# Two MLPs behind linear attention on one core: pair order, hosted heads and weight preparation rearranged

## The chip, the core and the metric

The kernel runs on one core of one Trainium2 chip. The metric is the device time of one execution in microseconds (us). Times are medians of several runs. The profile is of one execution, taken by the hardware profiler.

## What is computed

The reference, cut to what matters:

```python
def _attn_ref(q, k, v, g_norm):                       # (8 batches, 8 heads, 576, 64)
    kv = np.einsum('bhsd,bhse->bhde', k, v)
    out = np.einsum('bhsd,bhde->bhse', q, kv)
    rms = np.sqrt(np.mean(out * out, axis=-1, keepdims=True) + 1e-06)
    return out / rms * g_norm

def _moe_ref(x, w_in, w_out):                         # 4608 x 512, 512 x 2048, 2048 x 512
    h = x @ w_in
    g = np.where(h >= 1, h, np.where(h <= -1, 0.0, (h + 1) ** 2 / 4))
    return g @ w_out

def _moe2_ref(x, w_in, w_out):                        # the same sizes
    r = np.maximum(x @ w_in, 0.0)
    return (r * r) @ w_out

x = attn_out.transpose(0, 2, 1, 3).reshape(4608, 512)
return _moe2_ref(_moe_ref(x, ...), ...)
```

The weights arrive as 64-bit floats, and the kernel narrows them itself.

## The kernel before, in words

The 4608 tokens are nine blocks of 512. Blocks 0 to 7 are the first 512 tokens of each batch; block 8 collects the last 64 tokens of all eight. Each number is held as a high and a low part, so that one product takes three matmuls.

**The plain stage.** Blocks 0 to 4 of the first layer run one after the other. A block has 16 slices of the hidden width. Slice f is an `h_stage` (12 matmuls into `ph`, evicted to `u`), a `g_stage` (`u` split into the two parts of `gs`) and, two slices later, an `out_stage` (12 matmuls into `acc`). A slice has two hook steps, so block b has the steps 32b to 32b+31. The `hooks` table says which other work is issued at which step. Two kinds of work are hooked in.

* **Attention** of a later batch, by pairs of heads: `load_kv`, `load_q`, `kv_stage` (matmuls `pkv`), `t_stage` (a transpose into `qf`, split into `qT0` and `qT1`), two `o_stage` (matmuls `po` from `qT` and `kvbd`) and `r_stage` (matmuls `pr`, then the norm). Batch b is computed during block b-1. Of batches 5 to 7 the results go to DRAM (`xpd`, and `xrd` for block 8).
* **Weight preparation.** The later stage needs sums of weight quarters. A *unit* (`which`, `i`) makes them for one slice pair of one weight matrix in both layers: two raw loads, two `prep_narrow`, `prep_sums`, four `prep_split` for layer 2; `prep_join`, `prep_sums`, two `prep_split` for layer 1. On DVE that is 20 instructions. Each `prep_split` fills one tile `s`, and `pay` stores it to DRAM (`wsd`) from ACT's DMA queue. There are 16 units, and `keep_first` stores 23 more weight tiles from SP's queue in steps 14 to 58. The split tiles take turns in four buffers (`w1_12` to `w1_15`).

**The pair stage.** The other work is done two blocks at a time with seven products in place of eight: `PAIRS` lists (layer, first block), and block 8 of layer 2 follows alone. A pair has an in-phase (`ph`, 28 steps of 12 matmuls) and an out-phase (`po`, 56 steps of 6). Weights come back from `wsd` as tiles `ws`, one DMA each. `x2_jobs` load and split the next pair's inputs (`xr` to `x2`) during the out-phase. `HOSTED` says which pair also computes attention; `in_pair` holds those jobs by step.

What sets the order on an engine: the program is written in this order with hooks, and a scheduler orders it into one fixed list per engine. Each engine runs its list in order, and a DMA issue stands in the list of the engine that issues it. DMA completions use eight semaphores in turn (`DMAHW0` to `DMAHW7` in the waits of the program), so an issue waits for the earlier transfer on its semaphore.

Of the kernel before, what the change touches and what calls it, by code (L numbers as in the profile page):

```python
# [77 lines left out]
def linear_attention_rms_two_mlps(  # L78
# [42 lines left out]
    xp = ctx.enter_context(tc.tile_pool(name="xp", bufs=2 * KD))  # L121
# [12 lines left out]
    PAIRS = [(2, 0), (1, PLAIN), (2, 2), (1, PLAIN + 2), (2, 4), (2, 6)]  # L134
    EARLY = ((5, 0), (5, 1), (5, 2))
    HOSTED = {
        0: ((6, 0), (6, 2), (5, 3), (6, 1), (6, 3)),
        2: ((7, 0), (7, 2), (7, 1), (7, 3)),
    }
    hosted = [a for n in HOSTED for a in HOSTED[n]]  # L140
# [167 lines left out]
    prep_tags = itertools.cycle(range(NF - TAIL + RING + 2, NF))  # L308

    def prep_tile(name, shape, dtype):  # L310
        return wp.tile(shape, dtype, tag=f"w1_{next(prep_tags)}", name=name)
# [97 lines left out]
    def load_kv(b, hp):  # L409
        h0 = 2 * hp  # L410
        if b > 0:

            r = rests[turn[b, hp] % len(rests)]
            kvr[b, hp] = (r[:, 0], r[:, 1])
        both = None
        if (b, hp) in hosted[2:]:
# [211 lines left out]
    def new_x(L, b):  # L628
        xs[L, b] = [
            xp.tile([P, 2, TB], F32R, tag="x", name=f"x{L}_{b}_{c}") for c in range(KD)  # L630
        ]
# [137 lines left out]

    w_ring = Ring(*((wp, f"w1_{i}") for i in (0, 1, 2, 3, 4)))  # L770
    t_ring = Ring(*[(gp, "g")] * 3, (wp, f"w0_{NF - 2}"), (wp, f"w0_{NF - 1}"))
    g_ring = Ring(*[(xp, "x")] * 8, *((wp, f"w1_{5 + i}") for i in range(8)))
# [335 lines left out]
    jobs += attention(2 * NF * (PLAIN - 1), 9, EARLY)  # L1108
# [12 lines left out]

    kept = [(w, f) for f in range(NF) for w in range(2) if w == 0 or f < NF - TAIL]
# [3 lines left out]
    units = []  # L1126
    for n in range(NQ):
        for which, i, s in ((0, 2 * n, 0), (0, 2 * n + 1, 8), (1, n, 16), (1, n + NQ, 24)):
            units.append((which, i, 2 * NF * (n + 1) - 4 + 2 * n + s))
    units[-1] = (*units[-1][:2], 2 * NF * PLAIN - 7)  # L1130
    for which, i, s0 in units:
        for d, L, f, a in (
# [16 lines left out]
    last = 2 * (PLAIN - 1) * NF  # L1149
# [172 lines left out]
```

## Time and profile before

| | us |
|---|---|
| median of 3 runs | 1569.22 (1567.16 to 1569.58) |
| the profiled execution, own time | 1570.57 |
| its span, first to last instruction | 1568.8 |
| TensorE (PE) busy | 1537.6 |
| VectorE (DVE) busy | 1197.7 |
| ScalarE (ACT) busy | 932.2 |
| mean granted TensorE clock | 0.996 of full |

The plain blocks 1 to 4 start their first matmul at 128.1, 236.2, 335.9 and 433.7 us; the first matmul of the pair stage is at 536.1 us, its first out-phase starts at 630 us. PE, DVE, ACT and SP are engines; "PE po <- ACT qT" means that PE's matmul into `po` waited for ACT's write of `qT`. "L879" is line 879.

### The profile page before, as it was taken

To read this page: it belongs to the slowest core of one execution; us is meant where nothing else is said; L and a number is where in the kernel's file an instruction comes from. 1 tells how busy PE (TensorE), PEld (TensorE's weight loads), DVE (VectorE), ACT (ScalarE), POOL (GpSimd) and SP (SyncE) were. 2 spreads that over 40 slices of the span, in tenths; PEclk is the share of its full clock that TensorE was granted. 3 is DMA by queue.
4 is the path that set the end of the run, shared out by engine and by line. 5 is a ranking of instruction groups with operands and counts; after the bars stand their busy time and mean duration, and the time that the engine had idled before them with its cause. 6 is when DMAs were issued, how large, how long until landed. Compare 5 with 4: busy or idle time off the path is not lost.

```text
span 1568.8 us, 22366 instructions
## 1 busy us (share of the span) xinstructions
PE 1537.6 (98%) x7631; PEld 1268.9 (81%) x7633; DVE 1197.7 (76%) x2112; ACT 932.2 (59%) x1751; POOL 11.9 (1%) x30
## 2 busy tenths in 40 slices
PE   9999899999999999999999999999999999999999
PEld 5787678888777778788888888888888888888899
DVE  6987878887888767987897479878975597558666
ACT  5976766776757556754674466546743464446354
POOL 0000000000000000000000000000000000000000
PEclk9999999999999999999999999999999999999999
DMA  9677999787897977778677867696776676977796
GB/s 287 198 251 226 309 339 316 253 256 256 256 317 243 331 239 203 234 203 227 210 248 230 254 200 246 213 247 219 246 231 210 194 248 193 246 246 218 216 391 249
DMA packets 330914, 388.17 MB, mean 247 GB/s; under 512 B 197808, under 2 KB 223408, under 8 KB 330800
## 3 DMA queue, kind: packets, MB, share of 16 engines
q1 hardware_dynamic: 299904, 330.63, 69.7%
q10 hardware_dynamic: 30896, 56.11, 9.6%
q8 instruction: 61, 1.00, 0.2%
q14 instruction: 53, 0.43, 0.1%
HBM read 300.42 MB, written 86.25 MB: 246 GB/s over the span
## 4 chain that ended last, share of the span: by engine, by line
PE 77%; DMA 6%; DVE 2%; ACT 2%; SPq 0%; issue 0%; ACTq 0%; DVEq 0%
PE po L879 32%; PE ph L879 31%; PE ph L243 6%; PE acc L243 6%; DMA wsd<-s 3%; DMA wt<-wsd 1%; PE po L243 1%; DMA ws<-wsd 1%; PE pkv L488 1%; PE pr L610 1%; DMA rest<-in_v_dram 1%; DMA xr<-x1d 1%; DMA xr<-xpd 0%; ACT s L222 0%; DVE s L190 0%
## 5 line engine op out<-in xcount | busy, mean ns | idle before, releaser
L879 PE MATMUL ph<-x,ws 128*128 128x512 f32 (+1 forms) x2352 | 504.8, 374 | 4.6 <-DVE u L706 2.4
L879 PEld LDWEIGHTS ph<-x,ws 128*128 128x128 f32 x2352 | 417.2, 188 | 83.4 <-DVE u L706 2.8
L879 PE MATMUL po<-t,ws 128*128 128x512 f32 x2016 | 460.1, 390 | 0.0
L879 PEld LDWEIGHTS po<-t,ws 128*128 128x128 f32 x2016 | 378.8, 188 | 79.0 <-DVE t L808 0.4
L808 DVE TENSOR_TENSOR t<-g,t 128x512 fp32r<-128x512 f32 (+1 forms) x336 | 216.3, 649 | 91.8 <-ACT t L222 87.1
L222 ACT CAST t<-g 128x512 fp32r<-128x512 f32 (+1 forms) x336 | 195.9, 590 | 126.5 <-PE po L879 64.1
L243 PE MATMUL ph<-x,w 128*128 128x512 f32 x960 | 242.9, 397 | 2.2 <-DVE u L706 0.8
L243 PEld LDWEIGHTS ph<-x,w 128*128 128x128 f32 x960 | 179.5, 190 | 41.9 <-ACT w L222 2.0
L243 PE MATMUL acc<-gs,w 128*128 128x512 f32 x528 | 131.7, 394 | 4.5 <-DVE gs L235 2.2
L956 ACT ACTIVATE g<-h 128x512 f32<-128x512 f32 (+1 forms) x120 | 70.6, 589 | 90.5 <-DVE h L945 90.4
L243 PEld LDWEIGHTS acc<-gs,w 128*128 128x128 f32 x528 | 97.5, 188 | 26.2 <-DVE gs L235 2.6
L945 DVE CUSTOM_DVE_ANT_0 h<-ph,e 128x512 f32<-128x512 f32 (+1 forms) x120 | 76.4, 637 | 53.3 <-PE ph L879 49.4
L935 DVE TENSOR_TENSOR e<-ph,e 128x512 f32<-128x512 f32 (+1 forms) x112 | 72.1, 650 | 52.2 <-PE ph L879 47.2
L243 PE MATMUL acc<-gs,wt 128*128 128x512 f32 x432 | 106.2, 391 | 0.8 <-DMA wt<-wsd 0.8
L243 PEld LDWEIGHTS acc<-gs,wt 128*128 128x128 f32 x432 | 79.9, 188 | 17.6 <-DMA wt<-wsd 1.2
L222 ACT CAST x<-xr 128x512 fp32r<-128x512 f32 (+1 forms) x98 | 57.4, 590 | 49.8 <-DVE xr L859 30.3
L222 ACT CAST gs<-u 128x512 fp32r<-128x512 f32 x80 | 49.8, 622 | 46.2 <-DVE u L706 31.1
L706 DVE SCALAR_TENSOR_TENSOR u<-u,ph 128x512 f32<-128x512 f32 x80 | 54.5, 681 | 21.6 <-ACT u L229 21.4
L235 DVE TENSOR_TENSOR gs<-u,gs 128x512 fp32r<-128x512 f32 x80 | 54.9, 686 | 20.8 <-ACT gs L222 20.6
L704 ACT ACTIVATE u<-ph,halfb 128x512 f32<-128x512 f32 x80 | 55.3, 691 | 19.5 <-PE ph L243 13.3
L932 ACT COPY e<-ph 128x512 f32<-128x512 f32 (+1 forms) x56 | 30.7, 554 | 58.1 <-PE ph L879 49.6
L808 DVE TENSOR_TENSOR x<-xr,x 128x512 fp32r<-128x512 f32 (+1 forms) x98 | 62.9, 647 | 0.0
(135 smaller groups left out, 1623.3 us busy)
## 6 DMA issues: line engine op xcount, KB each, us to landing
ws<-wsd SPq DMA_DIRECT2D x392, 512.0 KB, 4.3
wsd<-s ACTq DMA_DIRECT2D x96, 512.0 KB, 5.2
wt<-wsd SPq DMA_DIRECT2D x36, 512.0 KB, 5.3
raw<-in_moe_w_in_dram SPq DMA_DIRECT2D x32, 512.0 KB, 6.8
raw<-in_moe_w_out_dram SPq DMA_DIRECT2D x32, 512.0 KB, 6.7
xr<-x1d SPq DMA_DIRECT2D x36, 256.0 KB, 4.5
out_dram<-ov SPq DMA_DIRECT2D x142, 64.0 KB, 3.9
wsd<-w SPq DMA_DIRECT2D x17, 512.0 KB, 4.7
```

The lines of the kernel that those rows point to most:

```text
L222: return e.copy(dst, src)
L235: lo = engine(op + "_lo", phase).tensor_tensor(t[:, 1, :], src, t[:, 0, :].bitcast(F32), ALU.subtract)
L243: nc.tensor.matmul(dst, wt(a), xt(c), start=first and n == 0, stop=last and n == 2)
L488: nc.tensor.matmul(ps[s, d], lhs, rhs, start=c == 0, stop=c == MR)
L704: nc.scalar.activation(u, ps, AF.Relu, bias=halfb, scale=0.5)
L706: nc.vector.scalar_tensor_tensor(u, u, 1.0, ps, op0=ALU.min, op1=ALU.max)
L808: engine2(op + "_lo").tensor_tensor(t[:, 1, :], src, t[:, 0, :].bitcast(F32), ALU.subtract)
L879: nc.tensor.matmul(ps, wt(a), xt(c), start=first and n == 0 and i == 0, stop=last and n == len(lhs) - 1 and i == 2, skip_group_check=True,)
L932: nc.scalar.copy(e[i, 1], bank)
L935: nc.vector.tensor_tensor(e[i, p], bank, e[i, 1], ALU.add)
L945: nc.vector._custom_dve(TENSOR_ADD_SAT, out=h, in0=bank, in1=add, s0=float("inf"), s1=0.0)
L956: nc.scalar.activation(g, h, AF.Square)
```

## The change

Four things are rearranged; the arithmetic is the same.

```diff
-    xp = ctx.enter_context(tc.tile_pool(name="xp", bufs=2 * KD))
+    xp = ctx.enter_context(tc.tile_pool(name="xp", bufs=1))
...
-    PAIRS = [(2, 0), (1, PLAIN), (2, 2), (1, PLAIN + 2), (2, 4), (2, 6)]
-    EARLY = ((5, 0), (5, 1), (5, 2))
+    PAIRS = [(2, 0), (2, 2), (1, PLAIN), (1, PLAIN + 2), (2, 4), (2, 6)]
     HOSTED = {
-        0: ((6, 0), (6, 2), (5, 3), (6, 1), (6, 3)),
-        2: ((7, 0), (7, 2), (7, 1), (7, 3)),
+        0: ((5, 0), (5, 1), (5, 2), (5, 3), (6, 0), (6, 2)),
+        1: ((6, 1), (6, 3), (7, 0), (7, 1), (7, 2), (7, 3)),
     }
...
     def prep_tile(name, shape, dtype):
-        return wp.tile(shape, dtype, tag=f"w1_{next(prep_tags)}", name=name)
+        return prep_ring.tile(shape, dtype, name)
...
+    prep_ring = Ring(*((wp, f"w1_{i}") for i in range(NF - TAIL + RING + 2, NF)))
...
-    jobs += attention(2 * NF * (PLAIN - 1), 9, EARLY)
...
-    units = []
-    for n in range(NQ):
-        for which, i, s in ((0, 2 * n, 0), (0, 2 * n + 1, 8), (1, n, 16), (1, n + NQ, 24)):
-            units.append((which, i, 2 * NF * (n + 1) - 4 + 2 * n + s))
-    units[-1] = (*units[-1][:2], 2 * NF * PLAIN - 7)
-    for which, i, s0 in units:
+    units = (
+        ((0, 0, 4), (1, 0, 12), (1, 4, 20), (0, 1, 29)),
+        ((0, 2, 5), (1, 1, 14), (1, 5, 22), (0, 3, 30)),
+        ((0, 4, 6), (1, 2, 16), (1, 6, 24)),
+        ((0, 5, 0), (0, 6, 6), (0, 7, 12), (1, 3, 18), (1, 7, 25)),
+    )
+    hook(last + 1, prep_ring.add, *((xp, f"x{KD + i}") for i in range(KD)))
+    for which, i, s0, j in [
+        (which, i, 2 * NF * (n + 1) + s, 4 if s in (0, 6, 12) else 6)
+        for n in range(PLAIN - 1)
+        for which, i, s in units[n]
+    ]:
...
-            (6, 1, prep_join, ()),
-            (7, 1, prep_sums, ()),
-            (7, 1, prep_split, (2,)),
-            (8, 1, prep_split, (3,)),
+            (j, 1, prep_join, ()),
+            (j + 1, 1, prep_sums, ()),
+            (j + 1, 1, prep_split, (2,)),
+            (j + 2, 1, prep_split, (3,)),
...
-        for s, *job in sorted(attention(3 if n else 1, 7 if n else 6.5, HOSTED[n]), key=lambda j: j[0]):
+        for s, *job in sorted(attention(1, 6, HOSTED[n]), key=lambda j: j[0]):
```

* **Pairs.** Layer 2's blocks 0 to 3 go first, then layer 1's blocks 5 to 8. The first two pairs host six pairs of heads each, every 6 steps. Block 4 hosts no attention (before: three pairs of heads).
* **Units.** Before, the 16 units started at steps 28, 36, 44, 52 | 62, 70, 78, 86 | 96, 104, 112, 120 | 130, 138, 146, 153. Now they start at 36, 44, 52, 61 | 69, 78, 86, 94 | 102, 112, 120 | 128, 134, 140, 146, 153. The two raw loads of a unit are hooked six steps ahead of its start.
* **Buffers.** The eight x buffers get names, and from block 4 on the split tiles take turns in eight buffers, with the four x buffers that block 4 does not use.
* **After the last hosting pair** (now the second, before the third) the ring of weight tiles gets three more buffers and the ring of PSUM banks two more; that code is as it was.

What it does to the lists, at three places. First DVE's list in block 1, from the eviction `u` of slice 4 to the split `gs` of the same slice (`u_1_4` and `gs_1_4`; `d`, `s` and `j` are tiles of units, `pr` and `t` belong to attention). Before:

```order
L706 SCALAR_TENSOR_TENSOR u_1_4_1850<-u_1_4_1850,ph_1_4_1837 128x512
L365 TENSOR_TENSOR s_1_0_0_1666<-j_0_1629,j_8_1631 128x256
L368 TENSOR_TENSOR s_1_0_0_1666<-j_0_1629,s_1_0_0_1665 128x256
L596 TENSOR_TENSOR s2lo_0_1698<-wk_2_0_1576,s_2_0_1657 128x576
L190 TENSOR_TENSOR s_0_0_3_1701<-s_1_0_0_1666,s_0_0_3_1701 128x2x256
L275 TENSOR_SCALAR d_0_1_1705<-raw_0_1_1504 128x512
L235 TENSOR_TENSOR gs_1_3_1791<-u_1_3_1749,gs_1_3_1791 128x512
...
L532 TENSOR_TENSOR t_0_1767<-wk_2_0_1577,t_0_1767 128x576
L190 TENSOR_TENSOR s_0_1_1_1831<-d_0_9_1732,s_0_1_1_1831 128x2x256
L190 TENSOR_TENSOR s_0_1_2_1834<-s_2_0_1_1777,s_0_1_2_1834 128x2x256
L235 TENSOR_TENSOR gs_1_4_1859<-u_1_4_1850,gs_1_4_1859 128x512
```

The same place of the list now:

```order
L705 SCALAR_TENSOR_TENSOR u_1_4_1798<-u_1_4_1798,ph_1_4_1785 128x512
L274 TENSOR_SCALAR d_0_0_1655<-raw_0_0_1483 128x512
L234 TENSOR_TENSOR gs_1_4_1807<-u_1_4_1798,gs_1_4_1807 128x512
L275 SCALAR_TENSOR_TENSOR d_0_0_1655<-raw_0_0_1483,d_0_0_1655 128x512
L274 TENSOR_SCALAR d_0_8_1682<-raw_0_8_1485 128x512
L526 SCALAR_TENSOR_TENSOR t_0_1716<-pr_0_0_1707,t_0_1716 128x288
```

Before, 20 instructions stand between `u_1_4` and `gs_1_4`; now one does. From `u_1_0` to `u_1_8` the list has 95 instructions before and 72 now.

Second, ACT's list in block 4, from the eviction of slice 4 to that of slice 5 (`x` and `xr`: inputs of the first pair; `wsd`: stores of unit tiles). Before:

```order
L704 ACTIVATE u_4_4_4903<-ph_4_4_4890,halfb 128x512
L182 DMA wsd_0_3_117<-s_0_6_3_4859 128x2x512
L229 ACTIVATE u_4_4_4903<-u_4_4_4903 128x512
L222 CAST qT_5_1_4930<-qf_1_4929 128x576
L222 CAST s_0_6_2_4941<-s_1_0_6_4935 128x2x256
L222 CAST gs_4_4_4912<-u_4_4_4903 128x512
L222 CAST x_0_7_0_4944<-xr_0_12_4819 128x512
L704 ACTIVATE u_4_5_4963<-ph_4_5_4950,halfb 128x512
```

Now:

```order
L703 ACTIVATE u_4_4_4788<-ph_4_4_4775,halfb 128x512
L221 CAST x_0_5_0_4768<-xr_0_11_4706 128x512
L228 ACTIVATE u_4_4_4788<-u_4_4_4788 128x512
L221 CAST s_0_6_0_4798<-d_0_6_4737 128x2x256
L181 DMA wsd_0_2_108<-s_0_5_3_4733 128x2x512
L221 CAST gs_4_4_4802<-u_4_4_4788 128x512
L221 CAST s_0_6_1_4817<-d_0_14_4761 128x2x256
L221 CAST s_0_6_2_4820<-s_2_0_6_4792 128x2x256
L221 CAST x_0_7_0_4823<-xr_0_12_4708 128x512
L703 ACTIVATE u_4_5_4842<-ph_4_5_4829,halfb 128x512
```

The attention's `qT` is gone from there, the stores of unit tiles still stand between the evictions, and there are more unit tiles.

Third, PE's list where the first pair goes from its in-phase (`ph`) to its out-phase (`po_1_0`, `po_1_1`); `po_3_0`, and `po_0_0` now, are attention's (`qT`, `kvbd`). Before:

```order
L879 MATMUL po_1_1_6568<-t_1_0_6555,ws_1_0_1_6421 128x512 x3
L879 MATMUL po_1_0_6567<-t_1_1_6558,ws_1_0_1_6421 128x512 x3
L879 MATMUL po_1_1_6568<-t_1_1_6558,ws_1_0_1_6421 128x512 x3
L879 MATMUL po_1_0_6567<-t_1_2_6561,ws_1_1_1_6447 128x512
L879 MATMUL po_1_1_6568<-t_1_2_6561,ws_1_1_1_6447 128x512
L243 MATMUL po_3_0_6620<-qT_6_3_6544,kvbd_132 128x288
L243 MATMUL po_3_1_6649<-qT_6_3_6544,kvbd_132 128x288
```

Now:

```order
L879 MATMUL ph_5_7_6266<-x_0_3_1_5345,ws_0_3_3_6203 128x512 x3
L879 MATMUL po_1_0_6396<-t_1_0_6376,ws_1_0_1_6232 128x512 x3
L879 MATMUL po_1_1_6397<-t_1_0_6376,ws_1_0_1_6232 128x512
L242 MATMUL po_0_0_6387<-qT_6_0_6325,kvbd_131 128x288
L879 MATMUL po_1_1_6397<-t_1_0_6376,ws_1_0_1_6232 128x512 x2
L879 MATMUL po_1_0_6396<-t_1_1_6379,ws_1_0_1_6232 128x512
L242 MATMUL po_0_0_6387<-qT_6_0_6325,kvbd_131 128x288
```

A hosted `po` stands near the change of phase in both, of another pair of heads. Its four `pr` ahead of it are 26 matmuls and 10 small `pkv` away before, and 28 matmuls and 20 small `pkv` now. PE's list has 7287 matmuls in both programs (the trace shows those of plain fp32 twice).

## Rows read from the trace of the kernel before

**Rows 1.** The page, part 1: busy us, share of the span, instructions.

```profile
PE 1537.6 (98%) x7631; PEld 1268.9 (81%) x7633; DVE 1197.7 (76%) x2112; ACT 932.2 (59%) x1751; POOL 11.9 (1%) x30
```

**Rows 2.** Windows: length; busy PE, PEld, DVE, ACT, POOL; granted clock; DMA share, GB/s.

```profile
128.10:186.90 58.80, 52.83 (x254) 41.80 (x253) 45.91 (x87) 38.61 (x76) 0.94 (x2) 0.94 0.89 282
186.90:236.20 49.30, 47.37 (x271) 38.31 (x269) 38.07 (x74) 32.49 (x66) 0.74 (x2) 1.00 1.03 334
236.20:335.90 99.70, 99.56 (x528) 82.18 (x526) 82.65 (x158) 70.38 (x140) 1.66 (x5) 1.00 0.88 281
335.90:433.70 97.80, 95.54 (x469) 78.36 (x466) 78.01 (x146) 67.51 (x136) 0.71 (x3) 1.00 0.80 253
433.70:486.50 52.80, 49.30 (x251) 40.57 (x250) 43.74 (x83) 35.16 (x71) 2.51 (x1) 0.97 0.94 298
486.50:536.10 49.60, 48.16 (x267) 39.43 (x266) 42.53 (x81) 34.20 (x65) 0.00 (x0) 1.00 0.90 291
536.10:560.30 24.20, 19.77 (x87) 15.74 (x85) 14.41 (x27) 10.68 (x22) 0.00 (x0) 1.00 0.97 298
626.80:641.00 14.20, 11.77 (x63) 9.07 (x62) 11.35 (x20) 11.58 (x25) 0.00 (x0) 0.88 0.81 255
878.70:956.80 78.10, 78.10 (x393) 65.30 (x394) 56.76 (x95) 47.94 (x99) 0.00 (x0) 1.00 0.73 221
```

**Rows 3.** The chain that ended last: start, us, what.

```profile
1179.88 76.16 PE ph L879 x336
```

**Rows 4.** Timeline of PE, block 1: start, us, instruction, [idle before <-releaser].

```profile
171.51 2.10 PE L243 MATMUL acc<-gs,w 128*128 128x512 f32 x8 [2.21 <-DVE gs L235]
174.71 0.53 PE L243 MATMUL po<-qT,kvbd 128*128 128x288 f32 x2 [1.09 <-ACT qT L222]
```

**Rows 5.** Timeline of DVE and ACT, the same stretch.

```profile
170.78 0.68 DVE L235 TENSOR_TENSOR gs<-u,gs 128x512 fp32r<-128x512 f32 x1
173.19 0.77 DVE L567 STREAM_TRANSPOSE qf<-q 128x576 f32<-128x576 f32 x1
...
173.98 0.67 ACT L222 CAST qT<-qf 128x576 fp32r<-128x576 f32 x1 [3.20 <-DVE qf L567]
```

**Rows 6.** Timeline of PE and ACT, block 4.

```profile
472.93 0.53 PE L243 MATMUL po<-qT,kvbd 128*128 128x288 f32 x2 [3.50 <-ACT qT L222]
...
465.92 0.62 ACT L222 CAST x<-xr 128x512 fp32r<-128x512 f32 x1 [4.13 <-DVE xr L859]
...
471.69 0.63 ACT L229 ACTIVATE u<-u 128x512 f32<-128x512 f32 x1 [4.55 <-DMA xr<-x1d]
```

**Rows 7.** Lines of DVE in block 4, 433.7 to 536.1: count, busy us, mean ns.

```profile
L190 DVE TENSOR_TENSOR s<-s,s 128x512 fp32r<-128x512 f32 x16 | 11.0, 685 | 0.1
L276 DVE SCALAR_TENSOR_TENSOR d<-raw,d 128x512 int32<-128x512 int32 x8 | 5.4, 686 | 1.6 <-ACT raw L273 1.6
...
L275 DVE TENSOR_SCALAR d<-raw 128x512 int32<-128x512 int32 x8 | 3.1, 422 | 0.2
L528 DVE SCALAR_TENSOR_TENSOR t<-pr,t 128x288 f32<-128x288 f32 x6 | 2.4, 449 | 0.0
...
L623 DVE SCALAR_TENSOR_TENSOR t<-t,wk 128x576 f32<-128x576 f32 x3 | 2.3, 754 | 0.0
```

**Rows 8.** DMA in block 4, 433.7 to 536.1, and the page's unit stores.

```profile
DMA packets 28232, 30.19 MB, mean 295 GB/s; under 512 B 14908, under 2 KB 16956, under 8 KB 28225
...
wsd<-s ACTq DMA_DIRECT2D x96, 512.0 KB, 5.2
```

**Rows 9.** Timeline of DVE, first pair's start.

```profile
550.61 0.69 DVE L935 TENSOR_TENSOR e<-ph,e 128x512 f32<-128x512 f32 x1 [4.16 <-DMA wsd<-s]
```

**Rows 10.** Timeline of PE and ACT, first pair's change of phase.

```profile
636.36 0.53 PE L243 MATMUL po<-qT,kvbd 128*128 128x288 f32 x2 [1.93 <-ACT qT L222]
637.40 1.33 PE L243 MATMUL po<-qT,kvbd 128*128 128x288 f32 x4 [0.51 <-DVE qT L569]
...
633.61 1.25 ACT L222 CAST x<-xr 128x512 fp32r<-128x512 f32 x2 [0.36 <-DMA xr<-xpd]
```

More of the change, by code (lines that the diff above doesn't have):

```diff
@@ L133, in linear_attention_rms_two_mlps @@
     PLAIN = 5
-    PAIRS = [(2, 0), (1, PLAIN), (2, 2), (1, PLAIN + 2), (2, 4), (2, 6)]
-    EARLY = ((5, 0), (5, 1), (5, 2))
+    PAIRS = [(2, 0), (2, 2), (1, PLAIN), (1, PLAIN + 2), (2, 4), (2, 6)]
     HOSTED = {
-        0: ((6, 0), (6, 2), (5, 3), (6, 1), (6, 3)),
-        2: ((7, 0), (7, 2), (7, 1), (7, 3)),
+        0: ((5, 0), (5, 1), (5, 2), (5, 3), (6, 0), (6, 2)),
+        1: ((6, 1), (6, 3), (7, 0), (7, 1), (7, 2), (7, 3)),
     }
-    hosted = [a for n in HOSTED for a in HOSTED[n]]
+    in_ring = [a for n in HOSTED for a in HOSTED[n][2:]]
     xpd = {b: dr.tile([P, KD, TB], F32, name=f"xpd{b}") for b in range(PLAIN, B)}
@@ L307, in linear_attention_rms_two_mlps @@
     raw_tags = itertools.cycle((NF - TAIL + RING, NF - TAIL + RING + 1))
-    prep_tags = itertools.cycle(range(NF - TAIL + RING + 2, NF))
     def prep_tile(name, shape, dtype):
-        return wp.tile(shape, dtype, tag=f"w1_{next(prep_tags)}", name=name)
+        return prep_ring.tile(shape, dtype, name)
     prep = {}
@@ L415, in load_kv @@
         both = None
-        if (b, hp) in hosted[2:]:
+        if (b, hp) in in_ring:
             both = kv_ring.tile([P, 2, TB], F32, f"kv_{b}_{hp}")
@@ L629, in new_x @@
         xs[L, b] = [
-            xp.tile([P, 2, TB], F32R, tag="x", name=f"x{L}_{b}_{c}") for c in range(KD)
+            xp.tile([P, 2, TB], F32R, tag=f"x{b % 2 * KD + c}", name=f"x{L}_{b}_{c}")
+            for c in range(KD)
         ]
@@ L768, in tile @@
             return pool.tile(shape, dtype, tag=tag, name=name)
+    prep_ring = Ring(*((wp, f"w1_{i}") for i in range(NF - TAIL + RING + 2, NF)))
     w_ring = Ring(*((wp, f"w1_{i}") for i in (0, 1, 2, 3, 4)))
     t_ring = Ring(*[(gp, "g")] * 3, (wp, f"w0_{NF - 2}"), (wp, f"w0_{NF - 1}"))
-    g_ring = Ring(*[(xp, "x")] * 8, *((wp, f"w1_{5 + i}") for i in range(8)))
+    g_ring = Ring(*((xp, f"x{i}") for i in range(2 * KD)), *((wp, f"w1_{5 + i}") for i in range(8)))
     e_ring = Ring(*((ap1, t) for t in ("wk0", "wk1", "wk2", "hl0", "hl1")), (ap2, "q"))
@@ L1120, in linear_attention_rms_two_mlps @@
             hook(2 * (b * NF + f - 1) + 1, load_tail, b, f)
+    last = 2 * (PLAIN - 1) * NF
     kept = [(w, f) for f in range(NF) for w in range(2) if w == 0 or f < NF - TAIL]
@@ L1141, in linear_attention_rms_two_mlps @@
             (2, 1, prep_load, ()),
-            (6, 1, prep_join, ()),
-            (7, 1, prep_sums, ()),
-            (7, 1, prep_split, (2,)),
-            (8, 1, prep_split, (3,)),
+            (j, 1, prep_join, ()),
+            (j + 1, 1, prep_sums, ()),
+            (j + 1, 1, prep_split, (2,)),
+            (j + 2, 1, prep_split, (3,)),
         ):
             hook(min(s0 + d, 2 * NF * PLAIN - 1), f, L, which, i, *a)
-    last = 2 * (PLAIN - 1) * NF
     first_x = x2_jobs(0, Ring(*[(st, "st")] * 7))
@@ L1157, in linear_attention_rms_two_mlps @@
     for n in HOSTED:
-        for s, *job in sorted(attention(3 if n else 1, 7 if n else 6.5, HOSTED[n]), key=lambda j: j[0]):
-            if n == 0 and s == 0 and job[0] in (load_kv, load_q):
+        for s, *job in sorted(attention(1, 6, HOSTED[n]), key=lambda j: j[0]):
+            if s:
+                in_pair.setdefault((n, s), []).append(job)
+            elif n:
+                in_pair.setdefault((n - 1, 14 * NQ - 4), []).append(job)
+            else:
                 hook(last + 25, *job)
-            else:
-                in_pair.setdefault((n, s), []).append(job)
     nc.scalar.preload_act_table_set("natural_log_exp_and_others")
```

## Prediction

> **What bounds the kernel now.** The page comes first: PE is busy 98% of the span [rows 1]. Then the chain: a whole phase of a pair is 336 matmuls in 76.16 us, 227 ns each, without a gap [rows 3]. The change removes no matmul and adds none. So it can only give back time in which PE stands still or runs slowly, and the windows, cut at the block starts, show where that is [rows 2]. Length less PE's busy time is 5.97 and 1.93 us in block 1, 0.14 in block 2, 2.26 in block 3, 3.50 and 1.44 in block 4, 4.43 at the start of the first pair and 2.43 at its change of phase: 22.1 us. The granted clock adds to it: 0.94 over 58.8 us is 3.5 us lost, 0.97 over 52.8 us is 1.6, 0.88 over 14.2 us is 1.7. In each of these three windows PE had just stood still, and part of the time it then ran at the lower level (1.2 GHz). All together 28.9 us are there to win. The rest of the idle time lies ahead of 128 us or at the very end, where the change puts nothing new.
>
> Next the cause of each. In block 1 PE waits 2.21 us for `gs` and 1.09 us for `qT` [rows 4]; DVE reached them at 170.78 us and, for `qf`, at 173.19 us, while ACT stood 3.20 us for that `qf` [rows 5]. DVE is late by its own list: it is busy 45.91 of the 49.3 us of full-speed work that PE has there (52.83 less 3.5), 93% [rows 2]. In block 4 ACT is late: 4.13 us for DVE's `xr`, then 4.55 us with a unit's store in its list behind a transfer still in flight [rows 6]. At the first pair's start DVE waits 4.16 us for a store of a unit tile, whose buffer the `e` tile takes [rows 9]. At the change of phase `qT` is late by 1.93 and 0.51 us, with two casts of `x` ahead of it on ACT [rows 10].
>
> The windows give a scale of what DVE's load costs (DVE busy over PE's full-speed work) [rows 2]: at 80 to 83% (second part of block 1, blocks 2 and 3) 1.9, 0.1 and 2.3 us are lost; at 88% (second part of block 4) 1.4; at 92% (first part of block 4) 5.1; at 93% (first part of block 1) 9.5, the clock's part included.
>
> **Block 1.** A DVE instruction takes 0.528 us of engine time there (45.91 us for 87). From `u_1_0` to `u_1_8` the list shrinks from 95 instructions to 72, because the unit of step 28 is gone: 38 us of DVE against 49.3 of PE, 77%. By the scale that loses next to nothing, and `gs_1_4` now stands two places behind `u_1_4`, not 21. But the list is uneven. From `u_1_4` to `u_1_8` 57 of 64 instructions stay: 30 us against 21.8 us for four slices and some 3 us of attention matmuls. Two slices between `h_stage` and `out_stage` can hide most of this surplus of 5 us, not all. I leave 2.0 us of 9.5: **gain 7.5**. Bounds: 0, if the quarter decides, and 9.5. In the last four slices DVE goes from 31 to 52 instructions, 27 us against some 26 of PE; DMA, which moved 334 GB/s in this window at a share of 1.03, has one unit less. I leave 1.93 as it is: **0**, between a gain of 1.9 and a loss of 3.
>
> **Blocks 2 and 3.** Block 2 has four units as before, one of them begun in block 1: **loss 0.4**. Block 3 has three in place of four: **gain 0.8** of 2.26.
>
> **Block 4.** Three pairs of heads leave, a unit comes. A unit's 20 DVE instructions are 8 like L190 and L344 at 685 ns, 2 at 686, 2 at 422 and 8 quarter sums as short as the 422: 11.1 us as recorded [rows 7]; records of neighbours overlap, and by the window's mean (86.27 us for 164 instructions, 0.526) it is 10.5 us. A pair of heads has five of 754 ns, two of 449 and two small ones, nine instructions, 4.7 us; three are 14.2. So DVE has 86.3 + 10.5 - 14.2 = 82.6 us to do. PE then needs 384 x 227 ns = 87.0 us and 1.3 for two hosted `pkv`: 88.3. DVE stands at 94%, where the scale says 5 to 10 us lost, against 6.5 before (3.50 + 1.44 + 1.6). Against this stands that nothing of attention hangs between DVE, ACT and PE there any more: two of the three waits (`po`, and `pr` behind `s2lo`) have no one waiting. ACT's list is shorter, but the stores are still between `u` and `gs`, so a late transfer still holds ACT, and `u` waits behind it, and `ph` for its bank. Eight buffers in place of four for the split tiles take the tile waits away, not the stores' own. I take 4.5: **gain 2.0**, between a gain of 6.5 and a loss of 4.
>
> The added unit also moves eight transfers of 0.52 MB (two raw tiles, six tiles `s`), 4.2 MB; three pairs of heads moved 3.5 MB (q, k, v and the result, 128 x 576 fp32 each). Block 4 moved 30.2 MB [rows 8], so about 30.9 now. At 334 GB/s, which block 1 held over 49 us [rows 2], that is 92.5 us: 4.2 over PE's need, the same size as DVE's part and beside it. The Trainium skill, DMA: Bandwidth & Descriptors, section "Issuing engines are not separate DMA queues", says that transfers run on the same 16 DMA engines whichever engine issues them. By that rule the stores on ACT's queue make no bandwidth of their own, and the trace agrees: SP's and ACT's transfers together fill a share of 1.03 in block 1 [rows 2].
>
> **Start of the first pair.** The last unit starts at step 153 as before and ends clamped at 159. The `e` tiles still take buffers of its last tiles, and the four added buffers shift only which. Stores landed 5.2 us after issue in the median [rows 8]. Of 4.43: **gain 0.4**, between 2.5 and a loss of 2.
>
> **Change of phase.** Hosted `po` stands near it again, in both hosting pairs. In the first, 28 matmuls and a double `pkv` (about 7.6 us) lie between the previous `pr` and it, where before it was about 6.6, and no cast of `x` stands ahead of `qT0`. The next pair's inputs are now `x1d`, long stored, in place of `xpd`, which was just being written. I leave 0.8 of the 4.1 (2.43 and 1.7 of clock): **gain 3.3**, between 0 and 4.1. The second hosting pair gets the same place anew: **loss 0.7**, between 0 and 4.1. Its six pairs of heads every 6 steps load DVE more than the four every 7 before (56.76 us busy of 78.10, without a gap [rows 2]): two more pairs are 9.4 us, 85%, still on the harmless side of the scale.
>
> At nothing: the new names of the x buffers (the first pair's first tiles take x0 to x3, read last by block 4's `h_stage`; x4 to x7 hold the last unit's tiles, next written one round of 14 steps, 19 us, later, which covers a 5.2 us store); the raw loads, six steps (16 us) ahead of their use on SP as before; the move of `w_ring` and `ps_ring` additions to the third pair, where PE has no gap to lose.
>
> **Sum.** 7.5 + 0 - 0.4 + 0.8 + 2.0 + 0.4 + 3.3 - 0.7 = 12.9 us. The profiled execution took 1570.57 (span 1568.8), so 1557.7 for its like; the median of the runs lies 1.35 lower, so **1556.3 us**, 0.8% faster.
>
> **Rivals.**
> *Block 4 takes part back.* If its DVE load follows the scale to 10 us, or DMA gives only the 298 GB/s of its first part, where 30.9 MB need 103.7 us, it loses 10 to 15 us in place of 4.5: 1562 to 1567. For it: DVE at 94%. Against it: no attention chain there. Chance 0.17.
> *Slower.* One mechanism: DMA in block 4 falls behind, and ACT stands at its store issues. The change comes out over 0.2% (3.1 us) slower when block 4 loses 4.5 + 12.9 + 3.1 = 20.5 us, that is when it takes 109 us, which is 30.9 MB at 284 GB/s or less; the second part of block 4 moved 291 [rows 2]. There it was not always asked for more, so this speaks for it only in part; 334 in block 1 speaks against it. At 270 GB/s, 114 us: about 1575. Chance 0.11.
> *No change.* PE is the engine in demand, and the work that moves lies on others. The Trainium skill, Trace Analysis, section "Identifying the Most-Contended Engine", says that the engine with the most load is the one to optimize, and that matmul busy time says little of its headroom. By that rule alone the sum would be 0: 1569.2. The stalls speak against it: 22.1 us of PE idle with named waits [rows 2]. But if what is late only moves (DVE's last quarter of block 1, the second change of phase), the result is the same: 1566 to 1572. Chance 0.12.
> *Forecast*, 1548 to 1562: chance 0.60.
>
> The chances: faster by over 0.2% (which is about what a measurement of this kernel can tell from no change) 0.77, within 0.2% 0.12, slower 0.11. The range for 8 in 10 is 1548 to 1567: 1548 is block 1, block 4 and the change of phase near their best bounds, 1567 the first rival's end.
>
> **What would show it.** Right: PE idle in block 1's first part from 6 to about 2 us, with the clock at full; no `po` wait in block 4; waits of `ph` or `acc` for `u` and `gs` there, 4 to 5 us; short `po` waits at two changes of phase. Wrong: block 4 over 95 us long; a granted clock under 0.98 in it; new waits in block 1's last four slices or in the second pair.

## The result and the profile after

The changed kernel takes 1585.05 us (median of four runs, 1583.98 to 1586.7), the kernel before 1569.4 in the same comparison: a ratio of 1.0101, with a 95% interval of 1.0083 to 1.0118. It is 1.0% slower, where 0.8% faster was forecast, and the time lies outside the range. The profiled execution has a span of 1583.0 us against 1568.8.

The first fence is the windows of the changed kernel, cut as in [rows 2] at the starts of blocks and phases: length; busy PE, PEld, DVE, ACT, POOL; granted clock; DMA share, GB/s. In order they are the first part and the last quarter of block 1, block 4, the first pair's in phase, its change of phase and the rest of its out phase, and the second pair's in and out phase.

```profile
128.10:180.30 52.20, 49.64 (x254) 39.58 (x252) 33.76 (x63) 31.14 (x63) 3.42 (x2) 1.00 0.81 249
180.30:233.60 53.30, 48.40 (x271) 38.03 (x271) 40.39 (x78) 35.94 (x73) 0.74 (x2) 1.00 0.95 303
429.70:522.00 92.30, 90.91 (x426) 72.81 (x425) 80.00 (x153) 58.54 (x106) 0.00 (x0) 1.00 1.02 349
522.00:617.10 95.10, 92.65 (x482) 76.20 (x481) 64.32 (x109) 54.01 (x112) 0.00 (x0) 0.98 0.77 233
617.10:640.00 22.90, 22.87 (x107) 18.68 (x106) 22.29 (x39) 19.76 (x42) 0.00 (x0) 1.00 0.87 267
640.00:699.70 59.70, 57.68 (x253) 46.44 (x252) 53.03 (x87) 32.38 (x56) 0.00 (x0) 1.00 0.79 226
699.70:806.00 106.30, 92.80 (x498) 76.19 (x497) 59.17 (x99) 51.15 (x105) 0.00 (x0) 0.92 0.73 194
806.00:888.40 82.40, 80.14 (x357) 65.24 (x356) 73.96 (x123) 51.16 (x95) 0.00 (x0) 1.00 0.74 232
```

One row stands out: the second pair's in phase, 106.30 us long, of which PE is busy 92.80, at a granted clock of 0.92. The third pair of the kernel before, which hosts four pairs of heads, has nothing like it [rows 2]. In the same stretch DVE is busy 59.17 us and ACT 51.15, both far from full. The idle time is 13.5 us, and the clock costs about 6 more: the granted clock was at its lower level (1.2 GHz, 0.50 in the rows) twice, for 6.83 and 10.24 us, and fell during a wait both times. PE stood still for part of these stretches, which costs nothing more; it was busy in them for 3.75 and 7.67 us, so the half clock costs 1.9 and 3.8 us. The third row is the same phase of a run without the first pair's stores (below): the same 498 matmuls, no gap, full clock, 86.60 us of PE where they take 92.80 here.

```profile
724.17:731.00 6.83, 3.75 (x11) 3.08 (x12) 3.73 (x5) 1.99 (x5) 0.00 (x0) 0.50 0.89 244
754.89:765.13 10.24, 7.67 (x53) 6.29 (x54) 6.50 (x13) 3.38 (x10) 0.00 (x0) 0.50 0.26 93
...
699.60:786.20 86.60, 86.60 (x498) 71.85 (x497) 56.61 (x96) 50.92 (x105) 0.00 (x0) 1.00 0.80 221
```

What PE waits for there, from the view of waits (total us, times, longest):

```profile
PE po L242 <- ACT qT L221: 6.6, 1, 6.6
PE pkv L486 <- DVE t L526: 3.4, 1, 3.4
PE po L242 <- ACT kvbd L221: 1.4, 1, 1.4
```

The other 2.1 us are waits for `pr` (1.3) and for DVE's `qT` (0.8). The timelines of PE, ACT and DVE around the first of these waits (start, us, instruction, [idle before <-releaser]; one "..." between engines):

```profile
720.32 0.29 PE L608 MATMUL pr<-s2lo,ones 128*128 128x288 f32 x1
727.25 2.12 PE L242 MATMUL po<-qT,kvbd 128*128 128x288 f32 x6 [6.63 <-ACT qT L221]
...
720.45 0.89 ACT L609 ACTIVATE wk<-pr,lnb 128x288 f32<-128x288 f32 x2 [0.21 <-PE pr L608]
721.23 0.63 ACT L956 ACTIVATE g<-h 128x512 f32<-128x512 f32 x1
721.75 0.77 ACT L611 ACTIVATE wk<-wk,expb 128x576 f32<-128x576 f32 x1
722.55 0.68 ACT L228 ACTIVATE t<-wk 128x576 f32<-128x576 f32 x1
726.52 0.67 ACT L221 CAST qT<-qf 128x576 fp32r<-128x576 f32 x1 [3.29 <-DVE qf L565]
...
723.27 0.82 DVE L526 SCALAR_TENSOR_TENSOR t<-pr,t 128x288 f32<-128x288 f32 x2 [2.32 <-ACT t L228]
724.12 0.76 DVE L621 SCALAR_TENSOR_TENSOR t<-t,wk 128x576 f32<-128x576 f32 x1
724.92 0.76 DVE L622 TENSOR_TENSOR wk<-wk,t 128x576 f32<-128x576 f32 x1
725.71 0.78 DVE L565 STREAM_TRANSPOSE qf<-q 128x576 f32<-128x576 f32 x1
```

This is one chain, from `pr` of one pair of heads through ACT (log, exp, square) and DVE (the norm, then the transpose `qf` of the next pair of heads, which takes the buffer of `t`) and ACT again to `qT`. It takes 6.6 us. All three engines are idle for part of it, waiting for each other. It costs PE 6.63 us because nothing stands between its two ends in PE's list. These are the list's rows at that place (line, operation, out<-in; `pr_1` belongs to the pair of heads (6, 1), `po_3` to (6, 3)):

```
L608 MATMUL pr_1_1_7415<-s_6_1_7299,ones 128x288
L608 MATMUL pr_1_1_7415<-s2lo_1_7334,ones 128x288
L242 MATMUL po_3_0_7504<-qT_6_3_7431,kvbd_132 128x288
L242 MATMUL po_3_1_7533<-qT_6_3_7431,kvbd_132 128x288
```

In the first pair 28 to 39 matmuls of the pair (6.4 to 8.9 us at 227 ns) lie between such a `pr` and the next `po`. The second wait has the same form: `pr_3` of (6, 3) directly ahead of `pkv` of batch 7, which needs the PSUM bank that the norm reads, and with `po` directly behind, which needs `kvbd` (1.4 us). I call such a place a bunch. The kernel before has none in its pairs, the changed one has these two.

### The profile page after: what moved, and what is told of

Same layout as the page of the kernel before. It is cut to its first block, busy times and chain, and to the rows that moved or that the text cites. A ratio compares the mean times of both kernels' runs of the same rounds, so it can differ in the third digit from the quotient of the medians.

```text
span 1583.0 us, 22370 instructions
## 1 busy us (share of the span) xinstructions
PE 1542.7 (97%) x7631; PEld 1267.9 (80%) x7633; DVE 1196.0 (76%) x2112; ACT 930.2 (59%) x1751; POOL 13.0 (1%) x30
## 4 chain that ended last, share of the span: by engine, by line
PE 81%; DVE 7%; DMA 5%; ACT 4%; issue 1%; SPq 1%; ACTq 0%; DVEq 0%
PE ph L879 30%; PE po L879 30%; PE acc L242 9%; PE ph L242 8%; DMA wt<-wsd 2%; DMA wsd<-s 1%; PE po L242 1%; DMA ws<-wsd 1%; PE pkv L486 1%; DVE s L189 1%; PE pr L608 1%; DMA v<-in_v_dram 1%; DVE u L705 1%; DVE t L808 1%; DMA k<-in_k_dram 0%
```

## The experiments

All ratios are to runs of the kernel before made beside them, with 95% intervals. "The pair" is the second one, in phase plus out phase: 188.7 us in the changed kernel.

**Stores off SyncE's queue.** New in the second pair are the first pair's 32 stores (L1072), which now fall into a pair that hosts.

```
-            nc.sync.dma_start(dst, src)
+            (nc.scalar if a[0] == 0 else nc.sync).dma_start(dst, src)
```

> Edit: the 32 stores of the first pair's outputs, which fall into the second pair, are issued by ScalarE instead of SyncE; nothing else. In the changed kernel the in phase of the second pair takes 106.3 us (TensorE busy 92.8, clock 0.92) where four hosted heads took 84.3 in the kernel before, and TensorE's list there has pr of one pair of heads directly ahead of po of the next. Theory A (the list): the scheduler, with 32 stores queued on SyncE ahead of the weight tiles, puts the matmuls of the hosted heads back to back, and TensorE then waits for the chain through ScalarE and VectorE between them (6.6 and 3.4 us, and the clock that falls behind each). With the stores off that queue the list has 24 to 46 matmuls of the pair's own between them; the in phase falls to 84 to 88 us, all of it to 1563 to 1567 us. Rival B (bytes): the stores' bytes take the transfers' share in that stretch wherever they are issued; the time stays 1580 to 1585. Rival C (density): six hosted heads at every sixth step overload VectorE and ScalarE; the time stays 1580 to 1585.

Ratio 1.0032 (1.0018 to 1.0046), 1574.8 us. The list has no bunch and the two long waits are gone (the pair takes 179.0 us), but ACT stands at its own stores, four of them in 6.40 us, and PE behind it. The four issues themselves take 1.5 us of that; what ACT waits for between them stands in the last section. ACT's rows, then PE's:

```profile
727.11 6.40 ACTq L1072 DMA_DIRECT2D out_dram<-ov  x4
733.56 0.63 ACT L956 ACTIVATE g<-h 128x512 f32<-128x512 f32 x1 [7.90 <-DMA out_dram<-ov]
...
735.23 1.22 PE L879 MATMUL ph<-x,ws 128*128 128x512 f32 x2 [4.73 <-ACT e L932]
```

**No stores.** `put_out` of the first pair is skipped (`for h in range(4) if n`).

> Left out: the first pair's outputs (batches 0 and 1) are neither transposed nor stored. Theory A (the list): TensorE's list has the hosted heads spaced by 16 to 46 matmuls; the in phase of the second pair falls from 106.3 to 84 to 87 us, the whole to 1562 to 1566 us. Rival B (bytes): also back to 1562 to 1566, but then the run with the stores on ScalarE is not. Rival C (density): the stores had little to do with it; 1578 to 1585.

0.9975 (0.9962 to 0.9988), 1566.7 us; the in phase takes 86.6 us at full clock. As theory A has it, but it doesn't separate list from bytes.

**Other spacing.** `attention(3 if n else 1, 7 if n else 6, HOSTED[n])`.

> Edit: the six hosted pairs of heads of the second pair start at step 3 and come every 7 steps, the spacing at which the kernel before hosts four without a gap; the stores stay on SyncE. Theory A (the list): TensorE's list still has po, pr and the next po of the first two pairs of heads without a matmul of the pair's own between them, so most of the loss stays: 1575 to 1585 us, with a wait of 5 to 7 us for qT at the second pair of heads. Rival C (density): with a sixth more room the loss goes for the most part: 1563 to 1569. Rival B (bytes): nothing changes, 1583 to 1587.

1.0090 (1.0069 to 1.0111). The bunch `pr_1`, `po_3` is still in the list, and PE waits the same 6.63 us there, at 729.39 us; a second one, `pr` directly ahead of `pkv`, stands later, at 806 us (2.9 us). With more room between the heads the time is nearly the same, so density is not it.

**Stores later.** `i in ((13, 17, 21, 25) if n == 1 else (0, 1, 5, 9))`.

> Edit: the same 32 stores on SyncE in the second pair, behind steps 13, 17, 21 and 25 instead of 0, 1, 5 and 9. Theory A (the list): the list is now spaced for the first three pairs of heads and back to back later (pr of one directly ahead of pkv, and pr directly ahead of po, of heads 2 and 3 of the last batch), so the waits for qT and pkv move from the first third of the in phase to its last third; 1570 to 1583 us. Rival B (bytes): the loss moves with the stores too, but as waits for weight tiles, not for qT; Rival C (density): the waits stay at the first heads and the time stays 1583 to 1587.

1.0116 (1.0097 to 1.0135), 1588.4 us, slower than expected. The bunches moved in the list to the third and fourth heads of batch 7, and the waits moved with them:

```profile
784.04 0.69 PE L486 MATMUL pkv<-kv 128*64 128x64 f32 x16 [2.74 <-DVE t L526]
...
814.09 2.12 PE L242 MATMUL po<-qT,kvbd 128*128 128x288 f32 x6 [6.50 <-ACT qT L221]
```

**Stores on GpSimd**, as in the first edit with `nc.gpsimd`.

> Edit: the 32 stores of the first pair's outputs are issued by GpSimd, which has no work in the pairs; nothing else. With the stores on ScalarE the time came to 1574.8 us and the waits for qT were gone, but ScalarE stood 6.40 us at four of its own store issues and TensorE 4.73 us behind it; without the stores it was 1566.7 us. TensorE's list is nearly that without stores. Theory A (the list): the place of the stores in SyncE's queue made the list bad, the bytes did nothing: in phase of the second pair 84 to 89 us, the whole 1563 to 1569 us. Rival B (bytes): the remaining loss of the run with ScalarE came from the transfers themselves, in phase 94 to 97 us, the whole 1573 to 1577 us.

1.0234 (1.0201 to 1.0268), 1607 us: a miss. The list has no bunch and `qT` is waited for 0.2 us, but GpSimd issues a store only every 2.5 us or more (32 of them in 103 us), and a cast `t` on ACT had to wait until a store had left its buffer. ACT waits 26.05 us, PE 16.9 of them:

```profile
749.57 0.62 ACT L221 CAST t<-g 128x512 fp32r<-128x512 f32 x1 [26.05 <-DMA out_dram<-ov]
```

So the run says nothing against the list, and nothing for it. The Trainium skill, DMA: Bandwidth & Descriptors, section "Issuing engines are not separate DMA queues", says that another issuing engine saves only sequencer time, usually little next to the transfer. Here the same 32 stores gave 1.0032 from ScalarE and 1.0234 from GpSimd with no bunch in either list, and 0.9999 from SyncE where the list has none (a run below). The measurement decides: the choice was worth up to 2.3%, by the time between the issues and by what is queued behind them.

**Each half of the change alone.** First the new units with the order, early heads and hosting of before; then the order and hosting with the old formula for the units.

> Edit: the new places of the weight sums in blocks 1 to 4 (with the named x buffers and the ring that takes four of them), with the order of pairs, the early heads in block 4 and the hosting of the kernel before. Theory A: the plain part of the change does what was forecast, block 1 some 3 to 7 us shorter than before and the rest unchanged, and nothing is lost in the pairs, since the stores of the first pair fall into a pair that hosts nothing: 1560 to 1567 us. Rival D: the shorter plain stage of the changed kernel is only the three early heads moved out of block 4, and the sums are worth nothing: 1568 to 1571 us.

> Edit: the order of pairs and the hosting of the changed kernel, with the weight sums where the kernel before has them. Theory A: the second pair loses what it loses in the changed kernel (in phase 104 to 108 us, wait of 6 to 7 us for qT), and the gain of the sums is missing: 1586 to 1594 us. Rival D: the sums are worth nothing, and this is the changed kernel's time, 1583 to 1587. Rival E: the second pair's loss needs the new sums (by the buffers that they take or by what they leave late): 1560 to 1572.

The units alone: 1.0017 (1.0004 to 1.0031), no gain, where 1560 to 1567 us were expected: a miss. Block 1 is 2.9 us shorter, but block 4, which now has five units beside the three early pairs of heads, takes 110.70 us where it took 102.4 [rows 2], and PE waits for DVE's `u` (its window, columns as above, and a line of its waits):

```profile
429.70:540.40 110.70, 98.30 (x516) 78.41 (x515) 93.84 (x179) 72.22 (x143) 0.00 (x0) 1.00 0.95 310
```

```profile
PE ph L243 <- DVE u L706: 8.9, 4, 2.8
```

The order alone: 1.0146 (1.0127 to 1.0166), with the same waits in the second pair as the changed kernel (6.6, 3.4 and 1.4 us). So the loss comes with the order and its hosting; on top of it the units are worth 0.0045, 7 us.

**Eight and four heads.** (6, 1) and (6, 3) go to the first pair; batch 7 starts at step 20 of the second, every 7 steps.

> Edit: eight pairs of heads in the first pair (batches 5 and 6, every 6 steps), the four of batch 7 in the second pair from step 20 on, every 7 steps; the 32 stores stay on SyncE at steps 0, 1, 5 and 9. Theory A (the list): in the second pair TensorE's list has the hosted heads spaced, as the stores are issued before the first of them, and the bunch of one po and pr late in the first pair costs 3 to 8 us: 1564 to 1573 us. Rival B (bytes): the stores still meet the weight tiles, and the second pair's in phase is over 90 us without the attention in it: 1575 to 1585. Rival C (density): the first pair with eight pairs of heads loses as the second did with six, 1578 to 1590.

1.0115 (1.0096 to 1.0135): a miss in size. Late in the first pair, where none of the 32 stores is near, the list has `po` 12 matmuls behind a `pr` and then its own `pr` directly ahead of `pkv`; the second pair has another `pr` directly ahead of `pkv` (3.6 us). The first pair's out phase takes 99.1 us where it took 82.6. Two more pairs of heads are about 4.4 of that, so some 12 us are lost, not the 3 to 8 that I gave the bunch. From the last `pr` to `po` it was 9.2 us here, of which the 12 matmuls covered the smaller part. DVE is busy 85.18 us in this phase, about what PE needs for it at full clock (80.6 and 4.4), so rival C, whose 1578 to 1590 us hold the 1587.8, is not excluded by this run. The waits of PE late in the first pair, and the window of its out phase:

```profile
637.21 0.85 PE L242 MATMUL po<-qT,kvbd 128*128 128x288 f32 x2 [6.45 <-ACT qT L221]
...
641.51 0.61 PE L608 MATMUL pr<-s,ones 128*128 128x288 f32 x1 [1.83 <-ACT wk L213]
...
645.50 1.12 PE L486 MATMUL pkv<-kv 128*64 128x64 f32 x16 [2.67 <-DVE t L526]
...
618.00:717.10 99.10, 87.33 (x418) 71.70 (x417) 85.18 (x143) 62.56 (x122) 0.00 (x0) 0.93 0.75 210
```

**PE's order alone.** The loop over the second pair's in phase runs under a scheduler region that keeps PE's instructions in the order of the program; nothing else changes.

```
+        with tc.manual_schedule(engines={mybir.EngineType.PE}) if n == 1 else contextlib.nullcontext():
             for i, _ in enumerate(step_in):
```

> Edit: in the in phase of the second pair TensorE's list keeps the order in which the program emits it, where the scheduler chose it; stores (on SyncE), loads and hosting are those of the changed kernel. So far the loss went with the place of bunched heads in the list (runs with the stores late, without them, and with eight heads in the first pair), but each of those runs also moved stores or heads. Theory A (the list alone): the waits for qT (6.6 us) and pkv (3.4 us) and the clock behind them go; in phase 84 to 90 us in place of 106.3, the whole 1563 to 1570 us. Rival B (SyncE's queue on the chip): with 32 stores ahead of them the weight tiles come late, and TensorE, no longer given hosted matmuls to fill in, waits for weights: in phase 95 to 106 us, 1575 to 1586. The scheduler's order would then be right and only the place of the stores wrong.

> Edit: as the run with program order in the in phase of the second pair, and the same for its out phase. Theory A: as that run or up to 2 us faster, since the two waits for t at the start of the out phase (2.2 us) may go: 1562 to 1569 us. Rival B as there: 1575 to 1586.

In phase alone: 1.0035 (1.0017 to 1.0053), 0.0066 or 10 us better. The in phase takes 91.2 us, between the two theories, but hosted work moved from it into the out phase (90.3 us in place of 82.4), and the whole, 1576.3 us, lies at the lower end of rival B's range: theory A missed in size. What B predicted, PE waiting for weights, is 2.2 us only. The program has 36 matmuls ahead of `po_3`, and that wait is gone; but it puts `kv_stage` into the same step as the previous `r_stage`, so `pr` ahead of `pkv` stays (3.3 us). Both phases: 1.0061 (1.0043 to 1.0078), 1581.5 us, a miss too, with 1.6 us of waiting for weights; that list has a second `pr` ahead of `pkv`, late in the in phase (6.4 us for both).

**One bunch by hand**, with its twin. Both have no stores and program order; the first moves `o_stage` of (6, 3) from steps 10 and 11 to step 7.

```
+            if (n, job[0], *job[1:3]) == (1, o_stage, 6, 3):
+                s = 7
```

> Left out: transposing and storing the first pair's outputs (batches 0 and 1). TensorE's in phase of the second pair in program order, and in it po of the second pair of heads moved up by three and four steps, directly behind pr of the first: one bunch, made by hand, without any store near it. Against the same kernel without the bunch. Theory A (the list): TensorE waits 6 to 8 us there for qT, the clock falls behind it for 3 to 7 us, and the kernel is 8 to 12 us slower than the one without the bunch. Rival B (the stores or their queue make the wait): without stores the bunch costs 0 to 3 us.

> Left out: transposing and storing the first pair's outputs (batches 0 and 1). TensorE's in phase of the second pair in program order, no bunch in it: the twin of the run with one bunch. Theory A: 1562 to 1567 us, as the run without stores in the scheduler's order (1566.7). If program order itself costs something, it shows here: 1568 and more.

1.0065 (1.0043 to 1.0088) against 1.0024 (1.0007 to 1.0040): a difference of 0.0041. In the profiled executions the pair takes 186.4 and 176.6 us. The difference in the waits is one line, of the run with the bunch (the other has no such line):

```profile
PE po L242 <- ACT qT L221: 6.4, 1, 6.4
```

So a bunch makes the wait with no store about. Its cost is 6.4 us by the ratios, 8.6 by the medians (1582.05 and 1573.50 us) and 9.8 by the two profiled executions, where 8 to 12 were expected. The twin missed its 1562 to 1567 us: its list still has one bunch, `pr` ahead of `pkv`, which both runs share (3.3 us and the clock).

**No bunch.** The second pair's in phase in order of program as before, and the kv step one later, once with the stores and once without:

```
+            if n and job[0] == kv_stage:
+                s += 1
```

> Edit: TensorE's in phase of the second pair in program order, and the kv step of its hosted heads one step later, so that 12 matmuls lie between pr of one batch and pkv of the next; stores on SyncE as in the changed kernel. No bunch is left in the list. The run with program order alone gave 1576.3 us and still waited 3.3 us for the bank of pkv, with the clock at half behind it. Theory A: that second wait and its clock go, the kernel gains 5 to 8 us on that run: 1568 to 1572 us. Rival B (the stores' queue is what remains): the pkv wait goes but weights come later instead, 1574 to 1577 us.

> Left out: transposing and storing the first pair's outputs (batches 0 and 1). Otherwise the run without bunches (TensorE's in phase of the second pair in program order, kv one step later). With the stores it took 0.9999 of the kernel before, spread over 16 steps 1.0003. Theory A with a smaller second cost (the stores themselves, 3 to 5 us through SyncE's queue): 0.9965 to 0.998 of the kernel before, as the run without stores in the scheduler's order (0.9975). If the stores cost nothing once the list has no bunch, 0.999 to 1.000.

With the stores 0.9999 (0.9984 to 1.0014), 1570.4 us, without them 0.9993 (0.9982 to 1.0003). Left in the pair with the stores (174.5 us) are:

```profile
PE ph L879 <- DMA ws<-wsd: 3.1, 3, 1.9
PE po L879 <- DVE t L808: 2.3, 2, 1.8
PE po L242 <- DVE qT L567: 0.7, 1, 0.7
```

The whole slowdown of 0.0101 goes with the two bunches, and once they are gone the stores cost about 1 us, which these runs can't tell from nothing. The gain that was forecast does not come back with that: 0.9999 is no change. Without stores the scheduler's own order (0.9975) came out a little better than the pinned one (0.9993), though their intervals touch.

**Looking for more.** The stores two to a step under the scheduler's order (kv step one later); eight and four heads, every 5 and 8 steps, with spread stores; and the run without bunches with the stores spread, or with every second one on ScalarE.

```
+            for _ in range(2):
+                if waiting:
+                    nc.sync.dma_start(*waiting.pop(0))
```

> Edit: the scheduler chooses TensorE's order again; the 32 stores of the first pair are put on SyncE two to a step over 16 steps, where they came eight at once at four steps, and the kv step of the second pair's hosted heads is one step later. The list that the scheduler then makes has no bunch. Theory A: the bytes, the queue and the density are those of the changed kernel, and the 16 to 20 us are gone: 1565 to 1570 us. Rival B: no better than the run in program order without bunches, or worse, 1570 to 1577 us, for late weights.

> Edit: eight pairs of heads in the first pair, every 5 steps, and the four of batch 7 in the second from step 18 on, every 8; stores spread two to a step. The earlier run with eight and four had two bunches in its list and took 1587.8 us; this one has none. Theory A (the list): 1562 to 1570 us. Rival C (density): eight pairs of heads every 5 steps are denser than anything so far, VectorE and ScalarE fall behind in the first pair, 1575 to 1590 us.

> Edit: the run without bunches (TensorE's in phase of the second pair in program order, kv one step later), and the 32 stores on SyncE two to a step over 16 steps. That run took 1570.4 us and waited 3.1 us for weight tiles in the second pair; the run with the stores spread under the scheduler's order waited for none, but had pkv directly ahead of po (3.2 us for kvbd, 1.8 us for qT, the clock behind both) and took 1576.9. Theory A (the list, and the stores' place a smaller second cost): both waits go, 1566 to 1569 us. Rival B: spreading only moves the wait, 1570 to 1574.

> Edit: the run without bunches, and every second one of the 32 stores issued by ScalarE. Theory A: half as many stores ahead of the weight tiles, some 1.5 us of the 3.1 us wait go; ScalarE stands at its issues as it did with all 32 (6.40 us at four of them), for which TensorE then waits: 1569 to 1573 us. If ScalarE's stand is short with 16, 1566 to 1569.

1.0048 (1.0031 to 1.0066), 1.0069 (1.0042 to 1.0096), 1.0003 (0.9989 to 1.0017) and 1.0011 (0.9996 to 1.0027). The first two miss, since I had looked for one form of bunch only. Both lists have `pkv` directly ahead of `po`, which needs `kvbd`; and both have a place in the second pair with 24 matmuls (5.4 us) between `pr` and `po`, which cover the chain only in part (2.1 and 2.9 us are left). The other two are no better than the run without bunches: PE waits 0.3 and 1.2 us for weight tiles, not 3.1, but in the first of them 1.6 us for `kv`. Waits in the second pair of the first:

```profile
PE po L242 <- ACT kvbd L221: 2.2, 1, 2.2
PE po L242 <- ACT qT L221: 1.8, 1, 1.8
PE po L242 <- DVE kvbd L499: 1.0, 1, 1.0
```

No version that keeps the stores is measurably faster than the kernel before.

## Why the prediction was wrong

**The step that failed** is the end of "Change of phase": "The second hosting pair gets the same place anew: loss 0.7, between 0 and 4.1", with a DVE load of 85%, "still on the harmless side of the scale". The second and third pair together take 341.9 us (188.7 and 153.2) where they took 314.1; two hosted pairs of heads more account for about 4.4 (four cost 8.8 in the third pair of before), so some 23 us are lost, outside the bounds by far. DVE's load was not even high there: the in phase holds only four of the six pairs of heads, and DVE is busy 59.17 us against the 86.60 that PE needs at full clock, 68% and not 85. The scale compares sums over a stretch. It can't see that two ends of a chain of 6.6 us stand side by side in PE's list, and I looked at that list around the change of phase only, not over the pair. The rows were there to be read: PE's list is fixed before the chip runs it. Of the prediction's own signs of being wrong the last came true: new waits in block 1's last four slices and in the second pair.

**What is left without the bunches.** They are some 15 of the 23 us. In the run without bunches second and third pair take 326.9 us (174.5 and 152.4), 8.4 more than the 314.1 before and the 4.4 for the heads, and PE stands 6.4 us in the second pair: 3.1 for weight tiles, 2.3 for `t` at the change of phase, 1.0 for `qT`. With the stores left out and the scheduler's order the loss is 3.8 us, within the bounds. So 0.7 was too small a term even for a list without bunches, and this rest uses up what the other blocks gained.

**Why the scheduler made the bunches** is shown for the second pair only by what removes them: with the stores on another queue or gone the list has none, with the stores later they come later. That it counts on weight tiles coming late behind 32 stores, and fills PE with what it takes for ready, fits this but was not tested. In the run with eight and four heads a bunch arose where no such store is; its cause stays open.

**Point by point**, from lengths before and after, with 2.2 us for each hosted pair of heads that moved:
- Block 1, gain 7.5 forecast: 2.6. The first part went as forecast (6.0 us idle and 3.5 of clock down to 2.6 idle at full clock). The last quarter, forecast at 0 with a loss of 3 as its bound, is 4.0 us longer: idle 1.9 to 4.9 us, with PE waiting for `u` (2.8 us in four waits) and a weight tile (1.7), and 1.0 more of PE's busy time as recorded. The size is no accident of one execution: in the other runs with the new units block 1 takes 105.1 to 108.0 us, mostly under 106.
- Block 2, loss 0.4: 0.8. Block 3, gain 0.8: 2.2.
- Block 4, gain 2.0: 3.5. It loses 1.4 us, not 4.5, moves 349 GB/s and keeps full clock, so the rivals of block 4 fall, the one that was to make the kernel slower too (its 1575 us for a block of 114 us should by its own sum be about 1578). DVE at 88% of PE's time (80.0 of 90.9), not the 94% of the forecast, is back on the scale; with the early heads kept it is at 95%, and 12.4 us are idle, more than the scale's 5 to 10 (the run with the units alone).
- First pair, gain 3.7 (0.4 and 3.3): 1.7. The change of phase is without a stall, 22.90 us with 22.87 busy. Of the start 2.5 us of idle remain, and the out phase has 2.0 new.
- Together the first pair and the blocks gave 9.2 us where 13.6 were forecast (7.5 - 0.4 + 0.8 + 2.0 + 3.7): right in sign, two thirds in size.
- "No change" by the most-contended engine was wrong too: PE was that engine before and after, and its instructions were the same 7631; their order was worth 16 us.

So the forecast mechanism (DVE's load in the blocks) held in sign and in two thirds of its size, and a second one that it left out decided.

## What to carry to other kernels

When a change moves work that one engine shares with a chain over others, read the changed list of that engine over the whole stretch, and count at each place the work that stands between a chain's two ends: here 36 matmuls, 8.2 us, covered a chain of 6.6 us but for 1.2 us at most in the in phases (2.5 in one out phase); 24, 5.4 us, covered it in three places of one run and left 1.5 to 2.9 us in three others; where none stood between, PE waited for all of it, and the clock behind the two bunches cost about half as much again (6.2 us on 13.5 idle). The count is a guide and no rule: the chain's length changes with what else DVE and ACT have in their lists, 9.2 us in the run with eight and four heads. Where a scheduler sets the order, a change of DMAs can reorder matmuls; a load summed over a stretch does not show that. Before blaming bytes or load, keep everything and pin the order of that one engine: it is a few lines, and here it told the two apart, once the kv step, which the program itself put badly, was moved too.

## What the runs showed of the hardware

One store of 64 KB takes about the same to issue on each engine: 0.32 to 0.79 us on ScalarE, 0.65 to 0.89 on GpSimd, eight in a row in 6.49 us on SyncE. What differs is the time between issues.

On ScalarE the four issues in 6.40 us took 0.37, 0.33, 0.51 and 0.32 us. Three of them began 0.02 us after a weight tile that SyncE had asked for landed on the same semaphore, at 727.09, 730.18 and 733.17 us. So through the semaphores that they share, a store in ScalarE's list waited for SyncE's loads, and ScalarE's own work waited behind it. The fence shows the issues of the run on ScalarE (shortest, median and longest in ns), two pieces of its chain and SyncE's eight in the changed kernel:

```profile
L1072 ACTq DMA_DIRECT2D out_dram<-ov x32: 322/597/787, 695.5 to 748.8; - x32
...
727.20 5.97 DMA ws<-wsd
...
733.19 0.32 ACTq L1072
...
705.69 6.49 SPq L1072 DMA_DIRECT2D out_dram<-ov  x8
```

On GpSimd the stores went one at a time: each of the 31 later ones was issued 0.30 or 0.31 us after the one before it had landed. One landed 2.2 us after its issue at best, which makes the 2.5 us:

```profile
717.61 0.74 POOL L1072 DMA_DIRECT2D out_dram<-ov  x1 [1.81 <-issue]
720.15 0.74 POOL L1072 DMA_DIRECT2D out_dram<-ov  x1 [1.80 <-issue]
```

The waits cost the clock as well. The granted clock went to its lower level (1.2 GHz) during the wait of 6.6 us and stayed there for 3.75 us of PE's work behind it, and again during the wait of 3.4 us, for 7.67 us of work, with PE standing 1.4 us once more among them. A stretch at half clock costs half of PE's busy time in it, not half of its length: PE's standing still in it is in the idle time already. That makes 5.7 us for the two, and PE's busy time was 6.2 us longer than in the run without stores.
